# Causal attention and two MLPs on one core: a new order inside each pair of heads, and small [128 x 3..7] operations moved from VectorE to GpSimd

## The chip, the cores and the metric

The kernel runs on one core of one Trainium2 chip. The metric is the device time of one execution in microseconds (us). "Faster" or "slower" below is against the kernel before on the same chip.

## The reference

```python
scores = scale * np.matmul(q, k.transpose(0, 1, 3, 2))      # 2 x 12 heads, 448 x 448, head size 64
scores = np.where(mask, -1000000000.0, scores)              # causal
scores = scores - np.max(scores, axis=-1, keepdims=True)
attn = np.exp(scores)
attn = attn / (np.sum(attn, axis=-1, keepdims=True) + 1e-09)
attn_out = np.matmul(attn, v)
x = attn_out.transpose(0, 2, 1, 3).reshape(896, 768)
h = np.maximum(x @ w_in, 0.0);  x = h * h @ w_out            # 768 -> 2048 -> 768
h = x @ w_in2;  out = (h - np.tanh(h)) @ w_out2              # 768 -> 2048 -> 768
```

## The kernel before

**Attention.** The 24 heads are worked in 12 pairs (`NPAIR`). A pair `n` puts its two heads on the two halves of the 128 partitions. The 448 queries are cut into seven blocks `c` = 0 to 6 of 64; by causality block `c` has 64(c+1) keys. A pair goes through these steps, each a helper function:

- `scores(n, t)`, TensorE, in two parts. For pairs from 1 on, part 0 holds blocks 6, 5, 0 and part 1 blocks 3, 2, 4, 1 (`STEPS`); each part fills two PSUM banks. A bfloat16 product with `maskb` adds the causal mask (L281).
- `maxes(n, t)`, VectorE: one `tensor_reduce` per block (L292, minus the row maximum, into the small tile `st`), then one multiplication of the three or four maxima by 0.125 (L294). ScalarE's exponential reads that as its bias.
- `exps(n, t, z)`, ScalarE: `prob = exp(0.125 s + bias)` and the row sums (L301).
- `recips(n)`, VectorE: 1e-9 is added to the seven sums (L305), then the reciprocals (L306). `norms(n, cs)`, VectorE: each block of `prob` times its reciprocals, in place (L313).
- `transposes(n, t)`, t = 0 to 3: four 128x128 transposes on TensorE into one of two PSUM banks `t` (L321), and a ScalarE copy into `pt` (L322). By `TBLK`, t = 0 reads blocks 0 to 3, t = 1 blocks 4, 5, 6 and then 2, t = 2 blocks 3 to 6, t = 3 blocks 4, 5, 6, 6.
- `pv(n, kcs)`, TensorE: products with V for key chunks 0 to 3 (L334). `xhi` on ScalarE and `xlo` on VectorE split the result into a rounded part and a rest (L347, L351).

**The order is written out by hand.** Every engine executes its own instructions in the order in which the helpers are called; waits between engines come from the data. The loop over `s` (L463 on) works on three pairs at once: scores of pair `s`, softmax of pair `p = s - 1`, transposes and products of pair `a = s - 2`. Then a tail without a loop finishes pairs 10 and 11 between the first groups of matrix products of the first MLP (`first(0, 0, m, 0)`).

**Weight preparation.** The float64 weights arrive as 64-bit words and are turned into two float32r parts by four VectorE operations on 128x768 (L113, L118, L123, L132 or L134) and two on ScalarE (L103, L125) per unit. `one()` issues the next of these VectorE operations if the budget of the pair (`SHARE_PAIR`, 800) is not used up; it is called twice a pair. `late()` issues the ScalarE operations that they leave behind.

**The MLPs** follow: groups of 128x128 by 128x448 matrix products in three passes (L364 to L366), with the weights prepared along the way.

Of the kernel before, what the change touches and what calls it, by code (L numbers as in the profile page):

```python
# [8 lines left out]
F32 = mybir.dt.float32  # L9
# [13 lines left out]
P = 128  # L23
# [5 lines left out]
NQ = S // D  # L29
# [33 lines left out]
def body(ctx: ExitStack, tc: tile.TileContext, qT, kT, vL, w1, w2, w3, w4, out):  # L63
    nc = tc.nc
    sb = ctx.enter_context(tc.tile_pool(name="sb", bufs=1))
    ps = ctx.enter_context(tc.tile_pool(name="ps", bufs=1, space=PSUM))
# [7 lines left out]
    def slot(i, shape, dt, name):  # L74
        return sb.tile(shape, dt, tag=f"slot{i}", name=name)
# [75 lines left out]
    def room():  # L151
        i = len(taken) - RING
        return i < 0 or taken[i] < freed[0]
# [10 lines left out]
    def late():  # L164
        while act_late:
            act_late.pop(0)()

    def one():

        if todo and budget[0] > 0 and (room() or not todo[0][3]):  # L170
            take()
            return True

    def take():
        f, cost, _, _ = todo.pop(0)
        f()
        budget[0] -= cost
# [19 lines left out]
    def load_qk(n):  # L197
        if n < NPAIR:
            b, hp = divmod(n, NP)
            qk[n] = (tmp(f"q{n}"), tmp(f"k{n}", "w"))  # L200
            nc.sync.dma_start(out=qk[n][0], in_=qT[b, hp])
            (nc.scalar if n == 0 else nc.sync).dma_start(out=qk[n][1], in_=kT[b, hp])

    def load_v(b):
        t = sb.tile([P, 3, DM], F32, tag=f"v{b}", name=f"v{b}")
        nc.sync.dma_start(out=t, in_=vL[b, : 3 * P].rearrange("(t p) d -> p t d", p=P))
        if b == 0:
            vs["end"] = slot(7, [D, B, DM], F32, "vend")
            nc.sync.dma_start(out=vs["end"], in_=vL[:, 3 * P :].rearrange("b p d -> p b d"))
        vs[b] = [t[:, 0], t[:, 1], t[:, 2], vs["end"][:, b]]  # L210
# [5 lines left out]
    def warm(count):  # L216
        o = ps.tile([P, 512], F32, tag="o", bufs=2, name="warm")[:, :S]
        for _ in range(count):
            nc.tensor.matmul(o, lhsT=ones[:, :P], rhs=ones, start=True, stop=True)  # L219
# [33 lines left out]
    sc = {}  # L253
    stat = {}
    pt = {}
    ob = {}

    def step(n, t):

        return STEPS[1 - t if n == 0 else t]  # L260

    def scores(n, t):
        q, k = qk[n]
        banks = []
        for z, cs in enumerate(step(n, t)):
            bank = ps.tile([P, 512], F32, tag="s", bufs=4, name=f"s{n}_{t}_{z}")
            banks.append(bank)
            for c in cs:
                sc[n, c] = bank[:, SOFF[c] : SOFF[c] + D * (c + 1)]
        for i in range(2):  # L270
            for z, cs in enumerate(step(n, t)):
                for c in cs[i : i + 1]:
                    for j in range(2):
                        r, e = slice(D * j, D * j + D), D * (j ^ z)
                        nc.tensor.matmul(sc[n, c][e : e + D], lhsT=q[r, D * c : D * c + D], rhs=k[r, : D * (c + 1)], start=(c == cs[0]), stop=False, skip_group_check=True)  # L275
        for z, cs in enumerate(step(n, t)):
            d = [SOFF[c] // D + c for c in cs]
            o = banks[z].rearrange("p (b k) -> p b k", k=D)[:, d[0] : d[-1] + 1 : max(d[-1] - d[0], 1)]
            for j in range(2):
                r, e = slice(D * j, D * j + D), D * (j ^ z)  # L280
                nc.tensor.matmul(o[e : e + D], lhsT=identb[r, r], rhs=maskb[r, : len(cs)], start=False, stop=True, skip_group_check=True)  # L281
        if t == 1:
            qk.pop(n)
            load_qk(n + 3)

    def maxes(n, t):
        if t == 0:
            stat[n] = sb.tile([P, 3, 8], F32, tag="stat", bufs=3, name=f"st{n}")
        st = stat[n]
        cs = [c for b in step(n, t) for c in b]  # L290
        for c in cs:
            nc.vector.tensor_reduce(out=st[:, 0, SI[c] : SI[c] + 1], in_=sc[n, c], axis=AX.X, op=ALU.max, negate=True)  # L292
        a, z = SI[cs[0]], SI[cs[-1]] + 1
        nc.vector.tensor_scalar_mul(out=st[:, 0, a:z], in0=st[:, 0, a:z], scalar1=0.125)  # L294

    def exps(n, t, z):
        st = stat[n]
        for c in step(n, t)[z]:
            w = D * (c + 1)
            i = SI[c]  # L300
            nc.scalar.activation(prob[n % 3][:, POFF[c] : POFF[c] + w], sc.pop((n, c)), AF.Exp, bias=st[:, 0, i : i + 1], scale=0.125, accum_out=st[:, 1, i : i + 1])  # L301

    def recips(n):
        st = stat[n]
        nc.vector.tensor_scalar_add(out=st[:, 1, :NQ], in0=st[:, 1, :NQ], scalar1=1e-9)  # L305
        nc.vector.reciprocal(out=st[:, 2, :NQ], in_=st[:, 1, :NQ])  # L306

    def norms(n, cs):
        st = stat[n]
        for c in cs:  # L310
            i = SI[c]
            p = prob[n % 3][:, POFF[c] : POFF[c] + D * (c + 1)]
            nc.vector.tensor_scalar_mul(out=p, in0=p, scalar1=st[:, 2, i : i + 1])  # L313

    def transposes(n, t):
        if t == 0:
            pt[n] = slot(3 + n % 2, [P, 16, P], F32, f"pt{n}")
        bank = ps.tile([P, 512], F32, tag="t", bufs=2, name=f"t{n}_{t}")
        for i, (kc, c) in enumerate(TBLK[4 * t : 4 * t + 4]):
            o = bank.rearrange("p (i j q) -> p i j q", j=2, q=D)[:, i, :: -1 if c in TURNED else 1]  # L320
            nc.tensor.transpose(o, prob[n % 3][:, POFF[c] + P * kc : POFF[c] + P * kc + P], ident)  # L321
        nc.scalar.copy(out=pt[n][:, 4 * t : 4 * t + 4], in_=bank.rearrange("p (i q) -> p i q", q=P))  # L322

    def pv(n, kcs):
        b, hp = divmod(n, NP)
        if 0 in kcs:
            ob[n] = ps.tile([P, 512], F32, tag="o", bufs=2, name=f"o{n}")
        o = ob[n]
        for kc in kcs:
            r = P if kc < 3 else D  # L330
            m = NQ - 2 * kc
            for j in range(2):
                h = 2 * hp + j
                nc.tensor.matmul(  # L334
                    o[D * j : D * j + D, P * kc : S],
                    lhsT=vs[b][kc][:r, D * h : D * h + D],
                    rhs=pt[n][:r, TBASE[kc] : TBASE[kc] + m, D * j : D * j + D],
                    start=(kc == 0),
                    stop=(kc == 3),
                    skip_group_check=True,  # L340
                )
        if 3 in kcs:
            pt.pop(n)

    def xhi(n):
        b, hp = divmod(n, NP)
        nc.scalar.copy(out=x[hp][:, 0, b], in_=ob[n][:, :S])  # L347

    def xlo(n):
        b, hp = divmod(n, NP)  # L350
        nc.vector.tensor_sub(out=x[hp][:, 1, b], in0=ob.pop(n)[:, :S], in1=x[hp][:, 0, b])  # L351
# [111 lines left out]
    for s in range(NPAIR):  # L463
        p, a = s - 1, s - 2
        sp, sa = p >= 0, a >= 0
        budget[0] = min(budget[0], 0) + (SHARE_PAIR if s > 1 else 0)
        if sa:
            transposes(a, 0)
        if sp:
            maxes(p, 1)  # L470
            exps(p, 1, 0)
        if sa:
            transposes(a, 1)
        if sp:
            exps(p, 1, 1)
        one()
        if a >= 1:
            xhi(a - 1)
        scores(s, 0)
        maxes(s, 0)  # L480
        if sp:
            recips(p)
            norms(p, (3, 2))
        if s == 2:
            warm(5)
        if a >= 1:
            xlo(a - 1)
        if sa:
            transposes(a, 2)
            transposes(a, 3)  # L490
        exps(s, 0, 0)
        exps(s, 0, 1)
        if sp:
            norms(p, (1, 0, 4, 5, 6))
        if sa:
            pv(a, (0, 1))
        late()
        scores(s, 1)
        one()
        if sa:  # L500
            pv(a, (2, 3))
        if s == 1:
            load_v(1)

    p, a = NPAIR - 1, NPAIR - 2
    budget[0] = min(budget[0], 0) + SHARE_LAST
    transposes(a, 0)
    maxes(p, 1)
    exps(p, 1, 0)
    transposes(a, 1)  # L510
    exps(p, 1, 1)
    one()
    xhi(a - 1)
    act = first(0, 0, 0, 0)
    recips(p)
    norms(p, (3, 2))
    xlo(a - 1)
    transposes(a, 2)
    transposes(a, 3)
    act()  # L520
    norms(p, (1, 0, 4, 5, 6))
    act = first(0, 0, 1, 0)
    pv(a, range(4))
    late()
# [5 lines left out]
    act = first(0, 0, 2, 0)  # L530
    for t in range(4):
        transposes(p, t)
    act()
    pv(p, range(4))
    late()
# [57 lines left out]
```

## Time and profile before

| | |
|---|---|
| time of the kernel before, median of 3 runs | 568.91 us (567.93 to 569.95) |
| time of the profiled execution | 567.94 us |
| its span, first to last instruction | 566.2 us |
| busy PE, DVE, ACT, POOL in the span | 553.8, 405.6, 336.8, 1.8 us |
| granted TensorE clock | 1.00 throughout |

The profile is of one execution. PE is TensorE, DVE VectorE, ACT ScalarE, POOL GpSimd. A row of a timeline gives start and duration in us, engine, line, operation, what it writes and reads, and how many equal instructions it merges ("x4"); in brackets the idle time of the engine before it and what ended it. The chain of waits follows the last instruction back to what released it, step by step. Instructions that follow each other on one engine overlap a little, so durations of single ones add up to more than the time they take together.

### The profile page before, as it was taken

To read this page: it belongs to the slowest core of one execution; us is meant where nothing else is said; L and a number is where in the kernel's file an instruction comes from. 1 tells how busy PE (TensorE), PEld (TensorE's weight loads), DVE (VectorE), ACT (ScalarE), POOL (GpSimd) and SP (SyncE) were. 2 spreads that over 40 slices of the span, in tenths; PEclk is the share of its full clock that TensorE was granted. 3 is DMA by queue.
4 is the path that set the end of the run, shared out by engine and by line. 5 is a ranking of instruction groups with operands and counts; after the bars stand their busy time and mean duration, and the time that the engine had idled before them with its cause. 6 is when DMAs were issued, how large, how long until landed. Compare 5 with 4: busy or idle time off the path is not lost.

```text
span 566.2 us, 8063 instructions
## 1 busy us (share of the span) xinstructions
PE 553.8 (98%) x3134; PEld 479.5 (85%) x3134; DVE 405.6 (72%) x727; ACT 336.8 (59%) x650; POOL 1.8 (0%) x11
## 2 busy tenths in 40 slices
PE   6899999999999999999999999999999999999997
PEld 3455558899999999999999999999999999999996
DVE  5889995588667527665648579998887499898511
ACT  4798896777654336666424258786565487864100
POOL 1000000000000000000000000000000000000000
PEclk9999999999999999999999999999999999999999
DMA  8732301245355514333133330110665311015211
GB/s 279 296 123 66 107 1 57 59 164 167 113 168 167 168 56 168 111 112 111 57 112 112 111 113 1 56 56 11 214 218 172 118 50 56 1 57 184 81 49 49
DMA packets 15525, 61.85 MB, mean 109 GB/s; under 512 B 1664, under 2 KB 6400, under 8 KB 15488
## 3 DMA queue, kind: packets, MB, share of 16 engines
q1 hardware_dynamic: 15200, 61.00, 32.5%
q8 instruction: 24, 0.39, 0.3%
q10 hardware_dynamic: 288, 0.34, 0.2%
q14 instruction: 13, 0.11, 0.1%
HBM read 58.59 MB, written 2.75 MB: 108 GB/s over the span
## 4 chain that ended last, share of the span: by engine, by line
PE 90%; ACT 8%; DVE 2%; issue 0%; DVEq 0%; ACTq 0%
PE o L364 14%; PE o L365 14%; PE h L364 14%; PE o L366 14%; PE h L366 14%; PE h L365 14%; ACT p L301 4%; ACT pt L322 3%; PE o L334 3%; PE s L275 2%; PE t L321 1%; DVE st L292 1%; PE warm L219 1%; ACT x L347 1%; DVE p L313 0%
## 5 line engine op out<-in xcount | busy, mean ns | idle before, releaser
L364 PE MATMUL o<-g,w 128*128 128x448 f32 x384 | 141.3, 368 | 0.0
L365 PE MATMUL o<-g,w 128*128 128x448 f32 x384 | 141.2, 368 | 0.0
L366 PE MATMUL o<-g,w 128*128 128x448 f32 x384 | 140.3, 365 | 0.0
L364 PEld LDWEIGHTS o<-g,w 128*128 128x128 f32 x384 | 71.9, 187 | 7.2
L366 PEld LDWEIGHTS o<-g,w 128*128 128x128 f32 x384 | 72.1, 188 | 6.9
L125 ACT CAST w<-raw 128x768 fp32r<-128x768 f32 x64 | 57.9, 904 | 33.3 <-DVE raw L123 33.2
L365 PEld LDWEIGHTS o<-g,w 128*128 128x128 f32 x384 | 72.1, 188 | 6.4
L103 ACT ACTIVATE raw<-raw 128x768 f32<-128x768 f32 x64 | 59.3, 926 | 23.9 <-DMA raw<-w 23.9
L364 PE MATMUL h<-y,w 128*128 128x448 f32 x192 | 70.5, 367 | 0.0
L364 PE MATMUL h<-x,w 128*128 128x448 f32 x192 | 70.4, 367 | 0.0
L366 PE MATMUL h<-x,w 128*128 128x448 f32 x192 | 70.0, 365 | 0.0
L366 PE MATMUL h<-y,w 128*128 128x448 f32 x192 | 69.7, 363 | 0.0
L365 PE MATMUL h<-x,w 128*128 128x448 f32 x192 | 69.5, 362 | 0.0
L365 PE MATMUL h<-y,w 128*128 128x448 f32 x192 | 69.3, 361 | 0.0
L123 DVE SCALAR_TENSOR_TENSOR raw<-raw 128x768 int32<-128x768 int32 x64 | 61.2, 956 | 1.3
L118 DVE SCALAR_TENSOR_TENSOR raw<-raw 128x768 int32<-128x768 int32 x64 | 61.0, 953 | 0.9 <-ACT raw L103 0.9
L134 DVE TENSOR_TENSOR w<-raw,w 128x768 fp32r<-128x768 f32 x32 | 30.6, 958 | 28.0 <-ACT w L125 27.9
L373 DVE TENSOR_TENSOR g<-r,g 128x448 fp32r<-128x448 f32 x32 | 20.0, 625 | 37.8 <-ACT g L370 37.8
L301 ACT ACTIVATE p<-s,st 128x256 f32<-128x256 f32 (+6 forms) x84 | 40.1, 511 | 8.1 <-DVE st L294 7.0
L132 DVE SCALAR_TENSOR_TENSOR w<-w,raw 128x768 fp32r<-128x768 f32 x32 | 30.7, 959 | 18.7 <-ACT w L125 18.5
L366 PEld LDWEIGHTS h<-y,w 128*128 128x128 f32 x192 | 35.9, 187 | 3.5
L366 PEld LDWEIGHTS h<-x,w 128*128 128x128 f32 x192 | 36.0, 187 | 3.0
(57 smaller groups left out, 742.7 us busy)
## 6 DMA issues: line engine op xcount, KB each, us to landing
raw<-w SPq DMA_DIRECT2D x64, 768.0 KB, 4.3
q<-qT SPq DMA_DIRECT2D x12, 224.0 KB, 4.6
k<-kT SPq DMA_DIRECT2D x11, 224.0 KB, 3.1
out<-part SPq DMA_DIRECT2D x11, 224.0 KB, 1.9
v<-vL SPq DMA_DIRECT2D x2, 1152.0 KB, 10.1
vend<-vL SPq DMA_DIRECT2D x1, 384.0 KB, 10.0
k<-kT ACTq DMA_DIRECT2D x1, 224.0 KB, 3.5
out<-part ACTq DMA_DIRECT2D x1, 112.0 KB, 1.7
```

The lines of the kernel that those rows point to most:

```text
L103: nc.scalar.activation(h, h, AF.Copy, scale=2.0**-112)
L118: nc.vector.scalar_tensor_tensor(out=lo, in0=hi, scalar=3, in1=lo, op0=ALU.logical_shift_left, op1=ALU.bitwise_or)
L123: nc.vector.scalar_tensor_tensor(out=lo, in0=hi, scalar=-0x80000000, in1=lo, op0=ALU.bitwise_and, op1=ALU.bitwise_or)
L125: act_late.append(lambda: nc.scalar.copy(out=st["w"][:, 0], in_=lo.bitcast(F32)))
L132: nc.vector.scalar_tensor_tensor(out=w[:, 1], in0=w[:, 0].bitcast(F32), scalar=-(1.0 - 2.0**-24), in1=f, op0=ALU.mult, op1=ALU.add)
L134: nc.vector.tensor_sub(out=w[:, 1], in0=f, in1=w[:, 0])
L301: nc.scalar.activation(prob[n % 3][:, POFF[c] : POFF[c] + w], sc.pop((n, c)), AF.Exp, bias=st[:, 0, i : i + 1], scale=0.125, accum_out=st[ ...
L322: nc.scalar.copy(out=pt[n][:, 4 * t : 4 * t + 4], in_=bank.rearrange("p (i q) -> p i q", q=P))
L364: nc.tensor.matmul(h, lhsT=hi, rhs=xh, start=(k == 0), stop=False)
L365: nc.tensor.matmul(h, lhsT=hi, rhs=xl, start=False, stop=False)
L366: nc.tensor.matmul(h, lhsT=lo, rhs=xh, start=False, stop=(k == kk - 1))
L373: nc.vector.tensor_sub(out=dst[1], in0=v, in1=dst[0])
```

## The change

Within a pair the calls are put in another order. All products with V of pair `a` come in one run behind both parts of the scores. `transposes` is split: `transposes` holds the TensorE part, `tcopy` the ScalarE copy, and the four exponentials of part 1 now stand ahead of the first two copies. The products of blocks 4, 5, 6 with their reciprocals (`norms(a, (4, 5, 6))`) move to the next turn of the loop, behind `maxes(p, 1)`; the other four stand together behind `recips(p)`. `late()` moves ahead of the exponentials of part 0. The multiplication of the maxima by 0.125 and the addition of 1e-9 to the sums go to GpSimd.

```diff
@@ maxes
-        nc.vector.tensor_scalar_mul(out=st[:, 0, a:z], in0=st[:, 0, a:z], scalar1=0.125)
+        nc.gpsimd.tensor_scalar_mul(out=st[:, 0, a:z], in0=st[:, 0, a:z], scalar1=0.125)
@@ recips
-        nc.vector.tensor_scalar_add(out=st[:, 1, :NQ], in0=st[:, 1, :NQ], scalar1=1e-9)
+        nc.gpsimd.tensor_scalar_add(out=st[:, 1, :NQ], in0=st[:, 1, :NQ], scalar1=1e-9)
@@ the loop over pairs
-        if sa:
-            transposes(a, 0)
         if sp:
             maxes(p, 1)
-            exps(p, 1, 0)
         if sa:
+            norms(a, (4, 5, 6))
+            transposes(a, 0)
             transposes(a, 1)
         if sp:
+            exps(p, 1, 0)
             exps(p, 1, 1)
+        if sa:
+            tcopy(a, 0)
+            tcopy(a, 1)
         one()
         if a >= 1:
             xhi(a - 1)
         scores(s, 0)
         maxes(s, 0)
+        if s == 2:
+            warm(5)
         if sp:
             recips(p)
-            norms(p, (3, 2))
-        if s == 2:
-            warm(5)
+        if sa:
+            transposes(a, 2)
+            tcopy(a, 2)
+            transposes(a, 3)
+            tcopy(a, 3)
+        if sp:
+            norms(p, (1, 0, 2, 3))
+        late()
+        exps(s, 0, 0)
+        exps(s, 0, 1)
         if a >= 1:
             xlo(a - 1)
+        one()
+        scores(s, 1)
         if sa:
-            transposes(a, 2)
-            transposes(a, 3)
-        exps(s, 0, 0)
-        exps(s, 0, 1)
-        if sp:
-            norms(p, (1, 0, 4, 5, 6))
-        if sa:
-            pv(a, (0, 1))
-        late()
-        scores(s, 1)
-        one()
-        if sa:
-            pv(a, (2, 3))
+            pv(a, range(4))
@@ the tail
+    maxes(p, 1)
+    norms(a, (4, 5, 6))
     transposes(a, 0)
-    maxes(p, 1)
+    transposes(a, 1)
     exps(p, 1, 0)
-    transposes(a, 1)
     exps(p, 1, 1)
+    tcopy(a, 0)
+    tcopy(a, 1)
     one()
     xhi(a - 1)
     act = first(0, 0, 0, 0)
     recips(p)
-    norms(p, (3, 2))
...
-    norms(p, (1, 0, 4, 5, 6))
+    norms(p, (1, 0, 2, 3, 4, 5, 6))
```

How the instructions stand now is shown at three places of the turn `s` = 8 of the loop, where `s8` are the scores of pair 8, `st8` and `st7` the small tiles of pairs 8 and 7, `p1` the probabilities of pair 7, `t6`, `pt6` and `o6` the transposes, their copy and the product of pair 6. Lines of the changed kernel are some higher: L292 is L293 there, L306 L307, L313 L314, L321 L320, L334 L338, L351 L355.

VectorE, from the sums of pair 7 to the reduces of part 1 of pair 8, before:

```order
L305 TENSOR_SCALAR st7_751<-st7_751 128x7
L306 RECIPROCAL st7_751<-st7_751 128x7
L313 TENSOR_SCALAR p1_127<-p1_127,st7_751 128x256
L313 TENSOR_SCALAR p1_127<-p1_127,st7_751 128x192
L351 TENSOR_TENSOR x5_72<-o5_781,x5_72 128x448
L313 TENSOR_SCALAR p1_127<-p1_127,st7_751 128x128
L313 TENSOR_SCALAR p1_127<-p1_127,st7_751 128x64
L313 TENSOR_SCALAR p1_127<-p1_127,st7_751 128x320
L313 TENSOR_SCALAR p1_127<-p1_127,st7_751 128x384
L313 TENSOR_SCALAR p1_127<-p1_127,st7_751 128x448
L292 TENSOR_REDUCE st8_845<-s8_1_0_880 128x1 x2
L292 TENSOR_REDUCE st8_845<-s8_1_1_881 128x1 x2
```

and now:

```order
L307 RECIPROCAL st7_751<-st7_751 128x7
L314 TENSOR_SCALAR p1_127<-p1_127,st7_751 128x128
L314 TENSOR_SCALAR p1_127<-p1_127,st7_751 128x64
L314 TENSOR_SCALAR p1_127<-p1_127,st7_751 128x192
L314 TENSOR_SCALAR p1_127<-p1_127,st7_751 128x256
L355 TENSOR_TENSOR x5_72<-o5_797,x5_72 128x448
L293 TENSOR_REDUCE st8_845<-s8_1_0_872 128x1 x2
L293 TENSOR_REDUCE st8_845<-s8_1_1_873 128x1 x2
L314 TENSOR_SCALAR p1_127<-p1_127,st7_751 128x320
L314 TENSOR_SCALAR p1_127<-p1_127,st7_751 128x384
L314 TENSOR_SCALAR p1_127<-p1_127,st7_751 128x448
L132 SCALAR_TENSOR_TENSOR w1_737<-w1_737,raw1_122 128x768
```

The three widest products stand behind the reduces of part 1 instead of ahead of them, and the addition (L305) is gone from this queue.

TensorE, from the last transposes of pair 6 to the first of pair 7 (left out are the mask products), before:

```order
L321 MATMUL t6_3_861<-ident_63,p0_126 128x128 x2
L334 MATMUL o6_875<-pt6_809,v1_235 64x448 x2
L334 MATMUL o6_875<-pt6_809,v1_235 64x320 x2
L275 MATMUL s8_1_0_880<-k8_613,q8_612 64x256 x2
L275 MATMUL s8_1_1_881<-k8_613,q8_612 64x320 x2
L275 MATMUL s8_1_0_880<-k8_613,q8_612 64x192 x2
L275 MATMUL s8_1_1_881<-k8_613,q8_612 64x128 x2
...
L334 MATMUL o6_875<-pt6_809,v1_235 64x192 x2
L334 MATMUL o6_875<-pt6_809,vend_114 64x64 x2
L321 MATMUL t7_0_903<-ident_63,p1_127 128x2x64 x2
```

and now:

```order
L320 MATMUL t6_3_858<-ident_63,p0_126 128x128 x2
L276 MATMUL s8_1_0_872<-k8_605,q8_604 64x256 x2
L276 MATMUL s8_1_1_873<-k8_605,q8_604 64x320 x2
L276 MATMUL s8_1_0_872<-k8_605,q8_604 64x192 x2
L276 MATMUL s8_1_1_873<-k8_605,q8_604 64x128 x2
...
L338 MATMUL o6_890<-pt6_828,v1_232 64x448 x2
L338 MATMUL o6_890<-pt6_828,v1_232 64x320 x2
L338 MATMUL o6_890<-pt6_828,v1_232 64x192 x2
L338 MATMUL o6_890<-pt6_828,vend_114 64x64 x2
L320 MATMUL t7_0_907<-ident_63,p1_127 128x2x64 x2
```

The first half of the products with V has moved behind part 1 of the scores.

GpSimd had nothing in the loop; its queue now, in the same turn (the first row is the part 0 of pair 8, the next the sums of pair 7):

```order
L295 TENSOR_SCALAR st8_845<-st8_845 128x3
L306 TENSOR_SCALAR st7_751<-st7_751 128x7
L295 TENSOR_SCALAR st8_845<-st8_845 128x4
L295 TENSOR_SCALAR st9_940<-st9_940 128x3
L306 TENSOR_SCALAR st8_845<-st8_845 128x7
```

The addition to the sums of pair 7 (L306) stands behind the multiplication of the part-0 maxima of pair 8 (L295).

## Rows read from the trace of the kernel before

**Rows 1.** Busy time by stretch: start:end, length, then PE, PEld, DVE, ACT, POOL.

```profile
28.35:83.91 55.56, 52.91 (x548) 30.17 (x544) 50.77 (x162) 49.32 (x159) 0.00 (x0) 1.00 0.24 76
107.70:566.20 458.50, 455.10 (x2232) 418.27 (x2231) 321.56 (x464) 254.67 (x402) 0.00 (x0) 1.00 0.32 106
```

**Rows 2.** Chain that ended last, in order of time: start us, us, what.

```profile
64.43 0.59 ACT pt L322
65.02 0.87 ACT p L301 x4
...
68.19 0.76 PE o L334 x4
...
71.34 0.59 ACT pt L322
...
93.68 2.03 PE o L334 x16
```

**Rows 3.** Timeline of VectorE over one pair.

```profile
61.82 1.43 DVE L313 TENSOR_SCALAR p<-p,st 128x128 f32<-128x128 f32 x5
63.17 1.27 DVE L292 TENSOR_REDUCE st<-s 128x1 f32<-128x256 f32 x4
64.47 0.17 DVE L294 TENSOR_SCALAR st<-st 128x4 f32<-128x4 f32 x1
64.55 0.95 DVE L132 SCALAR_TENSOR_TENSOR w<-w,raw 128x768 fp32r<-128x768 f32 x1
65.80 1.22 DVE L292 TENSOR_REDUCE st<-s 128x1 f32<-128x448 f32 x3 [0.30 <-PE s L281]
67.06 0.17 DVE L294 TENSOR_SCALAR st<-st 128x3 f32<-128x3 f32 x1
67.27 0.17 DVE L305 TENSOR_SCALAR st<-st 128x7 f32<-128x7 f32 x1
67.47 0.20 DVE L306 RECIPROCAL st<-st 128x7 f32<-128x7 f32 x1
67.70 0.58 DVE L313 TENSOR_SCALAR p<-p,st 128x256 f32<-128x256 f32 x2
68.20 0.61 DVE L351 TENSOR_TENSOR x<-o,x 128x448 fp32r<-128x448 f32 x1
```

**Rows 4.** Timeline of TensorE in the same pair: transposes, then part 0 of the scores.

```profile
63.68 1.09 PE L321 MATMUL t<-ident,p 128*128 128x128 f32 x8
64.70 0.99 PE L275 MATMUL s<-k,q 64*64 64x448 f32 x12
```

**Rows 5.** Groups by form, VectorE, 28.35 to 83.91: xcount | busy us, mean ns | idle.

```profile
L313 DVE TENSOR_SCALAR p<-p,st 128x448 f32<-128x448 f32 x9 | 4.0, 446 | 0.0
...
L313 DVE TENSOR_SCALAR p<-p,st 128x128 f32<-128x128 f32 x8 | 2.2, 276 | 0.0
L313 DVE TENSOR_SCALAR p<-p,st 128x64 f32<-128x64 f32 x8 | 2.0, 248 | 0.0
```

**Rows 6.** Groups by form, GpSimd, whole span (same columns).

```profile
L229 POOL TENSOR_SCALAR_AFFINE_SELECT maskb<-maskb 64x64 bf16<-64x64 bf16 x4 | 0.9, 237 | 0.1
...
L586 POOL MEMSET const-float32-1.0<- 128x1 f32 x1 | 0.1, 99 | 0.0
```

**Rows 7.** Timeline of the first pair: a small VectorE operation and the exponential behind it.

```profile
6.91 0.17 DVE L294 TENSOR_SCALAR st<-st 128x4 f32<-128x4 f32 x1
...
7.17 0.47 ACT L301 ACTIVATE p<-s,st 128x256 f32<-128x256 f32 x1 [4.50 <-DVE st L294]
```

**Rows 8.** Timeline: part-1 reduces of pairs 3 and 11; the first MLP's first product.

```profile
28.35 1.28 DVE L292 TENSOR_REDUCE st<-s 128x1 f32<-128x256 f32 x4
...
83.91 1.28 DVE L292 TENSOR_REDUCE st<-s 128x1 f32<-128x256 f32 x4
...
85.27 0.45 PE L364 MATMUL h<-x,w 128*128 128x448 f32 x1
```

More of the change, by code (lines that the diff above doesn't have):

```diff
@@ L255, in body @@
     pt = {}
+    tb = {}
     ob = {}
@@ L315, in transposes @@
     def transposes(n, t):
-        if t == 0:
-            pt[n] = slot(3 + n % 2, [P, 16, P], F32, f"pt{n}")
-        bank = ps.tile([P, 512], F32, tag="t", bufs=2, name=f"t{n}_{t}")
+        bank = tb[n, t] = ps.tile([P, 512], F32, tag="t", bufs=2, name=f"t{n}_{t}")
         for i, (kc, c) in enumerate(TBLK[4 * t : 4 * t + 4]):
@@ L321, in transposes, with tcopy @@
             nc.tensor.transpose(o, prob[n % 3][:, POFF[c] + P * kc : POFF[c] + P * kc + P], ident)
+    def tcopy(n, t):
+        if t == 0:
+            pt[n] = slot(3 + n % 2, [P, 16, P], F32, f"pt{n}")
+        bank = tb.pop((n, t))
         nc.scalar.copy(out=pt[n][:, 4 * t : 4 * t + 4], in_=bank.rearrange("p (i q) -> p i q", q=P))
@@ L515, in body @@
     recips(p)
-    norms(p, (3, 2))
     xlo(a - 1)
     transposes(a, 2)
+    tcopy(a, 2)
     transposes(a, 3)
+    tcopy(a, 3)
     act()
-    norms(p, (1, 0, 4, 5, 6))
+    norms(p, (1, 0, 2, 3, 4, 5, 6))
     act = first(0, 0, 1, 0)
@@ L532, in body @@
         transposes(p, t)
+        tcopy(p, t)
     act()
```

## The prediction

> **What bounds the kernel now.** I first read the busy time by stretch. From 107.7 us on TensorE is busy 455.10 of 458.50 us [rows 1]; the change touches nothing there, so that part only shifts. What can change is the attention, above all its regular part: from the part-1 reduces of pair 3 to those of pair 11 [rows 8] lie eight turns in 55.56 us, 6.95 us each, in which no engine is full (PE 52.9, DVE 50.8, ACT 49.3 us) [rows 1]. A loop of waits sets the pace. The chain in order of time shows which: it repeats every 6.91 us (64.43 to 71.34), and runs from the copy of a transpose through exponentials and copies on ScalarE into the products with V, through the scores, and back to the transposes [rows 2]. Last I read VectorE's timeline over one such pair: it has work nearly all the time, and waits 0.30 us for the scores [rows 3]. So the old loop passes through ScalarE and TensorE; VectorE has little slack.
>
> **What the change cuts.** In that chain the products with V stand between the copies and part 1 of the scores [rows 2]. Now they stand behind it, so the old loop is open: part 1 of the scores no longer waits for the last copies. If nothing else closed, the pace would fall to what the fullest engine needs: PE 52.9 / 8 = 6.6 us.
>
> **What it closes instead.** VectorE's new queue makes a longer loop. I walk it once from the first part-1 reduce, each step with its row:
>
> 1. Four reduces: 1.27 us to the end of the last; the next instruction overlaps some 0.05: 1.22 [rows 3].
> 2. Products of blocks 4, 5, 6, now right behind. Five products take 1.43 us from the first start [rows 3]; the two small ones among them last 276 and 248 ns [rows 5] and overlap what follows by 0.08 (61.82 + 1.43 = 63.25 against 63.17), so they hold the queue for 0.20 and 0.17. That leaves 1.06 to the end of the widest.
> 3. The second group of transposes reads blocks 4, 5, 6 and then 2, and part 0 of the scores stands behind it on TensorE. Its third transpose waits for the widest product. Two transposes are left: eight take 1.02 to the start of the scores [rows 4], so 0.26; with one hop of 0.09 between engines (6.91 + 0.17 = 7.08, next start 7.17 [rows 7]): 0.35.
> 4. Scores, from their start to the first part-0 reduce: 64.70 [rows 4] to 65.80 [rows 3], 1.10. The weight operation of `one()` (0.95) [rows 3] lies beside steps 3 and 4 (1.45) and costs nothing; were they shorter, it would cost what sticks out.
> 5. Three reduces: 1.22 [rows 3].
> 6. The reciprocals now wait for GpSimd. Its queue holds the multiplication of these maxima, then the addition to the sums. The sums are ready long before, but the addition is queued behind a multiplication that waits for step 5. So VectorE stands still for two GpSimd operations and two hops: 2d + 0.18.
> 7. Reciprocal to first product 0.23 [rows 3]; four products 0.87 (0.50 for two [rows 3], 0.20 and 0.17 as above); the rest `xlo`, 0.61 less the overlap, 0.53 [rows 3]. Then the next part-1 reduces start.
>
> The sum is 1.22 + 1.06 + 0.35 + 1.10 + 1.22 + 0.18 + 0.23 + 0.87 + 0.53 = 6.76, and 2d. **GpSimd's d is not in the trace.** Its bounds: a memset of one column, which reads nothing, 0.099 us, and an affine select of 64 columns, which reads, computes and writes as this does, 0.237 us [rows 6]. For 3 to 7 columns I take 0.20, nearer to the operation of the same kind. A turn is then 7.16 us against 6.95: +0.21, eight times: **+1.7 us** (0.0 at 0.10, +2.3 at 0.24; GpSimd may also take longer than either).
>
> What left VectorE is small: three operations of 0.17 us a pair hold it, with their waits, for 0.08 + 0.21 + 0.20 [rows 3]. Step 6 gives back more than that.
>
> **The way into the tail.** From the part-1 reduces of pair 11 to the first MLP product took 1.36 us (83.91 to 85.27) [rows 8]. Now steps 1 to 3 stand there, 1.22 + 1.06 + 0.35 = 2.63, since that product is queued behind the same transposes. TensorE needs it too: all sixteen products with V (2.03) [rows 2] and eight transposes (1.02) are left when the scores end. That is **+1.3 us**, once. Behind it TensorE is full in both kernels.
>
> **The way in.** Pairs 0 to 2 win up to half the products with V, 1.0 us, as part 1 of the scores comes ahead of them; and lose GpSimd's time in exponentials that nothing covers, and 0.95 in turn 2, where `one()` gives a second weight operation, which now stands in the loop. I take 0, between -0.8 and +0.7.
>
> **What costs nothing.** The copies moved behind the exponentials: from the part-1 reduces, multiplication 0.09 + 0.20 + 0.09, four exponentials in two rows of 0.87 and two copies of 0.59 [rows 2], the last four transposes and the scores come to about 1.2 + 0.4 + 1.7 + 1.1 + 0.6 + 1.1 = 6.1, one microsecond inside 7.16. ScalarE's `late()` ahead of the part-0 exponentials uses that too (49.3 / 8 = 6.2 us of work a pair). The loads of q and k are issued with part 1 of the scores, three pairs ahead, as before; no queue of the DMAs is passed. The product's PSUM bank has been free for a turn when it is needed.
>
> **Sum:** 1.7 + 1.3 + 0 = +3.0 us. The profiled execution took 567.94 us, so it would be 570.9; it was 1 us faster than the median of 568.91, so as a median 572.0 (+0.5%).
>
> **A port that two engines share.** The products with reciprocals take (446 - 248) / 384 = 0.52 ns a column [rows 5], while the subtraction `xlo`, also float32, takes 0.61 us for 448 [rows 3], over twice as much a column: products run at a doubled rate. The part-1 multiplication on GpSimd now starts just as three of them start. The Trainium skill, "SBUF — State Buffer", section "SBUF: two separate sides", has it that GpSimd and a VectorE operation in a mode with two ports, or with two SBUF inputs, lock a shared pair of ports for a whole instruction, and the other is blocked. No run here shows it. By that rule, with the lock free at the end of the first product, the multiplication waits some 0.4 us, inside the one of slack, and the sum stays; held from one instruction to the next it is the second rival.
>
> **Rivals.**
>
> - *GpSimd is quick and the way in wins* (no change). With d = 0.10 a turn takes 6.96: 0.1 for eight, + 1.3 - 0.8 = +0.6, 569.5. For it speaks the short memset; against it that no operation that reads is that short [rows 6]. Chance 0.15.
> - *GpSimd is kept out while VectorE runs one SBUF operation after the other* (slower by more). The part-1 multiplication waits until the three products and the weight operation are through: 1.22 + 1.06 + 0.87 = 3.15, instead of 1.3, after the first reduce. The path of the copies, 6.1, becomes 7.9 or 8.0: +1.0 a turn, 8 in all, + 1.3 = +9.3, 578.2. It decides from a delay of one microsecond on; if only the products hold it (1.0), the sum stands. For it: the instructions overlap, so there is no gap between them [rows 3]. Against it: two turns in eight have a shorter weight operation. Chance 0.17.
> - *The reciprocals don't wait, or hardly* (faster): GpSimd works on its two small operations at once and hops in 0.03, so that step 6 costs 0.1 in all and the transposes overlap the products. A turn takes 6.65, PE's own 6.6 being the floor: -0.3 x 8 = -2.4, + 1.3 - 0.8 = -1.9, 567.0. It decides where step 6 is below some 0.15. For it: the memsets' rows are close together; against it: the queue's order, which puts two operations in a row there. Chance 0.11.
>
> The forecast itself, with d from 0.15 to 0.35, has 0.57.
>
> **How the numbers follow.** The likeliest is 572.0; its own range is 570.5 to 575. A measurement of this kernel can tell about 0.3%, 1.7 us, from no change. The range is to hold 0.8: it leaves out the fast rival and the upper half of the blocked one, so 569.0 to 578.5. Slower by over 0.3%: the forecast (0.57), the blocked rival (0.17), less 0.02 for a small d: 0.72. Within: 0.15 + 0.02 = 0.17. Faster: 0.11.
>
> **What would show it.** VectorE idle ahead of the reciprocal in each turn, released by GpSimd's addition, about 0.5 us; idle ahead of the part-0 reduces of some 0.5 us, released by the scores; part-1 reduces waiting for nothing; the turn near 7.16 us; GpSimd's two lines near 0.2 us. It is wrong if the reciprocal never waits, if the turn falls under 6.9, or if the exponentials of part 1 start more than two microseconds after their reduces end.

## The result, and the profile after

The changed kernel takes 574.49 us (median of 4 runs, 573.36 to 575.47) against 568.77 for the kernel before (4 runs, 567.93 to 569.95): 1.0102 times as long, 95% interval 1.0084 to 1.012. It is slower, as forecast, and inside the range; but it lost 5.7 us where 3.0 were forecast. Of its four executions only the profiled one had a mean granted clock of 1.0; the other three had 0.994 to 0.997 and took 0.7 to 2.1 us more (the last section returns to this).

The profiled execution took 573.36 us with a span of 571.6, against 567.94 and 566.2: +5.42 in time. First the two ends of the regular part, by VectorE's and TensorE's timelines of the changed kernel: the first reduces of pair 0, the part-1 reduces of pairs 3 and 11, and the first MLP product.

```profile
6.13 2.44 DVE L293 TENSOR_REDUCE st<-s 128x1 f32<-128x256 f32 x7 [2.44 <-PE s L282]
...
29.15 1.27 DVE L293 TENSOR_REDUCE st<-s 128x1 f32<-128x256 f32 x4
...
88.16 1.27 DVE L293 TENSOR_REDUCE st<-s 128x1 f32<-128x256 f32 x4
...
90.66 0.45 PE L368 MATMUL h<-x,w 128*128 128x448 f32 x1
```

The eight turns take 59.01 us, 7.38 each, where they took 55.56, 6.95 each [rows 8]: **+3.45**. Pair 3 begins 0.80 us later (29.15 against 28.35). From pair 11 to the first MLP product lie 2.50 us instead of 1.36: **+1.14**. Together 5.39, all of the longer time but 0.03; from there on the two kernels run alike.

Busy time by stretch (columns as in [rows 1]) says that the loss is waiting and not work:

```profile
29.15:88.16 59.01, 53.42 (x544) 31.77 (x542) 46.75 (x138) 49.25 (x159) 8.43 (x24) 1.00 0.22 70
```

TensorE and ScalarE were busy for nearly as long as in [rows 1] (TensorE 0.5 us longer), VectorE 4.0 us less, in 3.45 us more.

One turn, walked as the prediction walked it. VectorE's timeline:

```profile
58.66 1.27 DVE L293 TENSOR_REDUCE st<-s 128x1 f32<-128x256 f32 x4
59.85 1.07 DVE L314 TENSOR_SCALAR p<-p,st 128x320 f32<-128x320 f32 x3
60.83 0.56 DVE L113 TENSOR_SCALAR raw<-raw 128x768 int32<-128x768 int32 x1
62.44 1.22 DVE L293 TENSOR_REDUCE st<-s 128x1 f32<-128x448 f32 x3 [1.05 <-PE s L282]
64.40 0.20 DVE L307 RECIPROCAL st<-st 128x7 f32<-128x7 f32 x1 [0.74 <-POOL st L306]
64.64 0.94 DVE L314 TENSOR_SCALAR p<-p,st 128x128 f32<-128x128 f32 x4
65.50 0.62 DVE L355 TENSOR_TENSOR x<-o,x 128x448 fp32r<-128x448 f32 x1
```

and TensorE's, second transposes and part 0 of the scores:

```profile
59.69 1.72 PE L320 MATMUL t<-ident,p 128*128 128x128 f32 x8
61.34 0.99 PE L276 MATMUL s<-k,q 64*64 64x448 f32 x12
```

The next part-1 reduces start at 66.03, so this turn has 7.37 us. In [rows 3] VectorE had two small operations and a reciprocal between the part-0 reduces and the products. Now it stands still there for 0.74 us, in every turn. The waits over the eight turns show this, and that VectorE's part-0 reduces wait for the scores and TensorE's transposes for VectorE's products (who waited for whom: us in total, times, longest; PEld is TensorE's weight load):

```profile
DVE st L293 <- PE s L282: 6.0, 8, 1.1
DVE st L307 <- POOL st L306: 5.9, 8, 0.7
PEld t L320 <- DVE p L314: 1.8, 8, 0.2
```

The chain in order of time shows what fills the 0.74 us (start, us, what):

```profile
62.46 1.21 DVE st L293 x3
63.67 0.02 issue
63.69 0.02 POOLq L295
63.71 0.10 issue
63.81 0.23 POOL st L295
64.04 0.08 issue
64.12 0.26 POOL st L306
64.38 0.02 issue
64.40 0.21 DVE st L307
```

The sums of the previous pair were ready long before; what VectorE waits for is GpSimd's queue, where their addition (L306) stands behind the multiplication of the maxima (L295) that have just been reduced. GpSimd by form (xcount | busy us, mean ns | idle):

```profile
L295 POOL TENSOR_SCALAR st<-st 128x4 f32<-128x4 f32 x12 | 6.3, 527 | 38.4 <-DVE st L293 38.4
L306 POOL TENSOR_SCALAR st<-st 128x7 f32<-128x7 f32 x12 | 3.0, 247 | 2.8 <-ACT p L302 1.9
L295 POOL TENSOR_SCALAR st<-st 128x3 f32<-128x3 f32 x12 | 2.8, 229 | 36.5 <-DVE st L293 36.5
```

Four columns take more than twice as long as three or seven. In pair 0, before any product, the 128x4 took 0.24 us; in ten of the other eleven 0.58. The timelines of GpSimd and ScalarE in the turn above:

```profile
60.01 0.58 POOL L295 TENSOR_SCALAR st<-st 128x4 f32<-128x4 f32 x1 [3.02 <-DVE st L293]
...
60.62 0.47 ACT L302 ACTIVATE p<-s,st 128x256 f32<-128x256 f32 x1 [0.87 <-POOL st L295]
```

It starts inside the first of VectorE's three widest products and ends at 60.59, right behind the second (60.55). The exponential that waits for it starts 0.03 later, so the long duration is no error of the record.

### The profile page after: what moved, and what is told of

It is laid out like the page before. It is cut to its first block, busy times and chain, and to the rows that moved or that the text cites. A ratio compares the mean times of both kernels' runs of the same rounds, so it can differ in the third digit from the quotient of the medians.

```text
span 571.6 us, 8095 instructions
## 1 busy us (share of the span) xinstructions
PE 556.5 (97%) x3134; PEld 482.4 (84%) x3134; DVE 399.7 (70%) x691; ACT 337.3 (59%) x650; POOL 13.8 (2%) x47
## 4 chain that ended last, share of the span: by engine, by line
PE 90%; DVE 5%; ACT 3%; POOL 1%; issue 1%; DVEq 0%; ACTq 0%; POOLq 0%
PE o L368 14%; PE o L369 14%; PE h L368 14%; PE o L370 14%; PE h L370 14%; PE h L369 13%; PE t L320 3%; DVE st L293 3%; PE o L338 2%; PE s L276 2%; ACT p L302 1%; DVE p L314 1%; ACT pt L326 1%; PE warm L219 1%; POOL st L295 1%
## 5 line engine op out<-in xcount | busy, mean ns | idle before, releaser
L320 PE MATMUL t<-ident,p 128*128 128x128 f32 x192 | 33.0, 290 | 9.2 <-ACT pt L326 5.3
```

## The experiments

The kernel before took 568.28 us beside e1 to e4, 568.63 beside e5 to e8 and 568.61 beside e9 and e10; ratios are against these. A turn is, as above, an eighth of the way from the part-1 reduces of pair 3 to those of pair 11. Diffs are against the changed kernel.

### Which of the two moved operations costs, and what the order costs alone

e1 puts the addition back on VectorE, e2 the multiplication, e3 both.

```diff
@@ e1, e3
-        nc.gpsimd.tensor_scalar_add(out=st[:, 1, :NQ], in0=st[:, 1, :NQ], scalar1=1e-9)
+        nc.vector.tensor_scalar_add(out=st[:, 1, :NQ], in0=st[:, 1, :NQ], scalar1=1e-9)
@@ e2, e3
-        nc.gpsimd.tensor_scalar_mul(out=st[:, 0, a:z], in0=st[:, 0, a:z], scalar1=0.125)
+        nc.vector.tensor_scalar_mul(out=st[:, 0, a:z], in0=st[:, 0, a:z], scalar1=0.125)
```

> The addition of 1e-9 goes back to VectorE, the multiplication stays on GpSimd. Queue theory (the reciprocals wait behind two GpSimd operations in a row, 0.74 us a turn in the changed kernel's trace): the wait goes, an addition of 0.20 comes, so a turn falls from 7.38 to 7.38 - 0.74 + 0.20 = 6.84 us and the time by 8 x 0.54 = 4.3 to about 570.2 us. Rival 1, the blocked multiplication of part 1 (0.58 instead of 0.23 us) and the exponentials behind it set the turn: the turn stays at 7.38 and the time at 574.5. Rival 2, the order alone is slow: the turn stays above 7.2 and the time above 573.

> The multiplication goes back to VectorE, the addition stays on GpSimd, where nothing stands ahead of it any more. Queue theory: no wait of the reciprocals; the two multiplications hold VectorE for 0.08 and 0.21 us a turn as in the kernel before: 7.38 - 0.74 + 0.29 = 6.93 us, time lower by 8 x 0.45 = 3.6, about 570.9 us. Rival 1 (exponentials behind a blocked GpSimd): also lower, the exponentials of part 1 start some 0.9 us earlier; e1 tells the two apart. Rival 2 (the order alone): above 573 us.

> The new order alone, nothing on GpSimd. Queue theory with the loop through VectorE as worked out: 7.38 - 0.74 + 0.29 + 0.20 = 7.13 us a turn, time lower than the changed kernel's by 8 x 0.25 = 2.0, about 572.5 us, so the order alone is some 0.2 us a turn slower than the kernel before. Rival 3 (all of the loss is GpSimd's): the turn is at or under 6.95 us and the time at or under 570.7 (the way into and out of the loop cost 1.9 us in the changed kernel).

Measured: e1 569.47 us (1.0019, 1.0010 to 1.0029), turn 6.81; e2 570.09 (1.0037, 1.0023 to 1.0050), turn 6.93; e3 573.05 (1.0087, 1.0072 to 1.0102), turn 7.14. VectorE's timeline of e1 at the reciprocals:

```profile
60.80 1.22 DVE L293 TENSOR_REDUCE st<-s 128x1 f32<-128x448 f32 x3 [1.12 <-PE s L282]
61.94 0.16 DVE L306 TENSOR_SCALAR st<-st 128x7 f32<-128x7 f32 x1
62.13 0.20 DVE L307 RECIPROCAL st<-st 128x7 f32<-128x7 f32 x1
62.37 0.94 DVE L314 TENSOR_SCALAR p<-p,st 128x128 f32<-128x128 f32 x4
```

The wait is gone, and with it 0.57 us of the turn: from the start of the reduces to the reciprocal it takes 1.33 us by way of VectorE's own addition, and took 1.96 by way of GpSimd. The three turns are within 0.03 us of those expected; the times of e1 and e2 lie 0.7 and 0.8 us below the expected ones, that of e3 0.6 above. e3 shows that the new order itself is 0.19 us a turn slower than the old one, and that moving both operations adds 0.24 to that. Against e3 each operation moved alone is a gain: 0.33 us a turn for the multiplications (e1) and 0.21 for the addition (e2), about what they hold VectorE in the loop (0.29 and 0.20). It is both together, in this order of the queue, that cost.

### Both on GpSimd, the addition ahead (e4)

```diff
-    def recips(n):
+    def sums(n):
         st = stat[n]
         nc.gpsimd.tensor_scalar_add(out=st[:, 1, :NQ], in0=st[:, 1, :NQ], scalar1=1e-9)
+
+    def recips(n):
+        st = stat[n]
         nc.vector.reciprocal(out=st[:, 2, :NQ], in_=st[:, 1, :NQ])
@@ the loop
         scores(s, 0)
+        if sp:
+            sums(p)
         maxes(s, 0)
@@ the tail
     act = first(0, 0, 0, 0)
+    sums(p)
     recips(p)
```

> Both stay on GpSimd, but the addition to the sums of pair p is queued ahead of the multiplication of the part-0 maxima of pair s; nothing else moves. Queue theory: the sums are ready 0.9 us before those maxima, so the wait of 0.74 us goes entirely: 7.38 - 0.74 = 6.64 us, or what then sets the turn: the path over the blocked multiplication, exponentials, copies, transposes and scores takes 65.24 - 58.66 = 6.6 us in the changed kernel's trace. So 6.65 to 6.85 us, time lower by 4.2 to 5.8: 568.7 to 570.3 us. Rival 1 (the blocked multiplication decides) and rival 2 (the order): 7.2 us a turn or more, 573 us or more.

Measured: 567.12 us (0.9979, 0.9969 to 0.9988), turn 6.68. The turn is as expected, the time 1.6 us below the expected range; in the profiled execution pair 3 begins at 28.37, not at 29.15. Timelines of VectorE and GpSimd:

```profile
59.05 1.22 DVE L293 TENSOR_REDUCE st<-s 128x1 f32<-128x448 f32 x3 [1.05 <-PE s L282]
60.19 0.19 DVE L310 RECIPROCAL st<-st 128x7 f32<-128x7 f32 x1
```

```profile
59.15 0.25 POOL L306 TENSOR_SCALAR st<-st 128x7 f32<-128x7 f32 x1 [1.94 <-ACT p L302]
60.43 0.31 POOL L295 TENSOR_SCALAR st<-st 128x3 f32<-128x3 f32 x1 [1.03 <-DVE st L310]
```

The addition starts under the reduces, 1.04 us ahead of the reciprocal, which follows the last reduce at once. The operations and their engines are those of the changed kernel, with durations that differ by less than 0.1 us in these rows (0.31 against 0.23 for the multiplication); what was changed is a place in a queue, and it is worth 0.7 us a turn. Against e3 the two moves now gain 0.46, near the sum of their single gains (0.54). This settles the term of step 6.

### What VectorE's operations do to GpSimd's (e5, e6, e9)

e5 keeps both operations on GpSimd and takes the order of the kernel before. There the part-1 multiplication falls beside a weight operation instead of the products.

```diff
@@ the loop, as before; maxes and recips as changed
+            transposes(a, 0)
         if sp:
             maxes(p, 1)
+            exps(p, 1, 0)
...
-            norms(a, (4, 5, 6))
-            transposes(a, 0)
...
             recips(p)
+            norms(p, (3, 2))
```

> The order of the kernel before, with the multiplication and the addition on GpSimd. Queue theory: the addition again stands behind the multiplication of the part-0 maxima, so the reciprocals start 0.15 + 0.23 + 0.08 + 0.25 + 0.03 = 0.74 us after the reduces where they started 0.45 us after them (67.02 to 67.47): +0.3 us a turn, of which VectorE's slack of 0.30 us hides most; and the part-1 multiplication runs beside a weight operation instead of three products. If that blocks it to the end of the weight operation (0.55 or 0.95 us), the exponentials of part 1, which are on the old loop's chain, start 0.3 to 0.7 us later. So 7.2 to 7.6 us a turn, 571 to 574 us. Rival 3 (GpSimd alone is the loss of the change, whatever the order): 6.95 + 0.43 = 7.38, 572 to 574.5 as well; rival (GpSimd costs nothing in the old order, as VectorE has slack there): 6.95, 568.3 us.

Measured: 576.54 us (1.0141, 1.0116 to 1.0166), turn 7.49: the turn is as expected, the time above it. Pair 3 begins at 31.52 in the profiled execution, 3.2 us later than before, with the granted clock at 0.62 and 0.53 in the rows from 14 to 18 us, and at 0.53 and 0.61 in those from 28 to 32 (more on this at the end). One turn in the timelines of VectorE, GpSimd and ScalarE:

```profile
69.92 0.95 DVE L132 SCALAR_TENSOR_TENSOR w<-w,raw 128x768 fp32r<-128x768 f32 x1
...
70.08 0.89 POOL L294 TENSOR_SCALAR st<-st 128x4 f32<-128x4 f32 x1 [4.00 <-DVE st L292]
...
71.01 0.47 ACT L301 ACTIVATE p<-s,st 128x256 f32<-128x256 f32 x1 [0.55 <-POOL st L294]
```

The multiplication starts 0.16 us after a weight operation with two SBUF inputs, whose record ends at 70.87, and lasts 0.89, to 70.97. In eleven turns it took 0.87 to 0.89 beside such an operation and 0.47 to 0.50 beside the shift L113 (0.56 us), and in pair 0, beside neither, 0.24. This is what the Trainium skill, "SBUF — State Buffer", section "SBUF: two separate sides", says of the pair of ports that the two engines share: whoever starts first has it for the whole instruction, and operations with two SBUF inputs count as well as those in a two-port mode. The trace agrees, with one addition: next to VectorE instructions that follow each other without a gap, GpSimd did get in (0.30 or 0.58 us beside three products of 1.07), so it was never kept out for a whole run of them.

e6 puts all seven products behind the reciprocals in the new order, so that the part-1 multiplication meets a weight operation there too; e9 does the same with the multiplication on VectorE.

```diff
@@ e6, e9
         if sa:
-            norms(a, (4, 5, 6))
             transposes(a, 0)
...
-            norms(p, (1, 0, 2, 3))
+            norms(p, (1, 0, 2, 3, 4, 5, 6))
@@ e9
-        nc.gpsimd.tensor_scalar_mul(out=st[:, 0, a:z], in0=st[:, 0, a:z], scalar1=0.125)
+        nc.vector.tensor_scalar_mul(out=st[:, 0, a:z], in0=st[:, 0, a:z], scalar1=0.125)
```

> All seven products stand together behind the reciprocals, none behind the part-1 reduces; there VectorE now does the weight operation at once. A test of the shared port: the part-1 multiplication on GpSimd, 0.58 us beside three products at double rate, should take 0.23 us where VectorE reads PSUM or rests, and last until the weight operation ends where one is running: some 0.5 us beside the shift (L113, 0.55 us, one input), 0.9 us beside those with two inputs (0.95 us) if they block it as well, 0.23 if they do not. If GpSimd's operation took 0.58 us for another reason than what runs beside it (its four columns, say), it stays at 0.58 in every turn. The turn is not the point: 6.9 to 7.7 us.

> All seven products behind the reciprocals, as in the run before with that order (turn 8.33 us, one look 583.0), with one thing changed: the multiplication of the maxima is on VectorE again, and the addition stays on GpSimd. If that order lost its time because GpSimd's multiplication lasts up to 0.88 us beside the weight operation and so holds up the exponentials, the copies behind them and the products with V: VectorE's multiplication comes right behind the reduces, before the weight operation, and the turn falls by 0.6 us or more, to 7.0 to 7.7, 573 to 578 us. If the order alone lost it (seven products ahead of the part-1 reduces, with TensorE and ScalarE waiting for them), the turn stays above 8.0 and the time above 580 us.

Measured, one execution each: e6 583.01 us, turn 8.33; e9 568.66 us, turn 7.10. In e6 GpSimd's multiplication took 0.87 to 0.88 us beside the weight operations with two inputs and 0.47 to 0.48 beside the shift, as expected if the port is locked; four columns as the reason for 0.58 is refuted. But e6's turn missed its expectation by far. e9's turn is in its expected range, its time 4 us below it. ScalarE's waits in the eight turns, e6 (waited for: us in total, times, longest):

```profile
ACT p L302 <- POOL st L295: 16.2, 7, 3.6
```

and e9:

```profile
ACT p L302 <- DVE st L295: 6.4, 6, 1.5
```

With the multiplication on GpSimd this order is 1.2 us a turn slower (8.33 against 7.10), and ScalarE, with its exponentials and all copies queued behind it, waits 9.8 us longer in eight turns. That is not the price of the multiplication alone. The addition again stands behind a multiplication in e6, and the granted clock falls four times within its eight turns (busy time in rows of 2 us; the column ahead of the last two is the clock):

```profile
42.00:44.00 2.00, 1.38 (x12) 1.06 (x16) 1.40 (x7) 2.00 (x7) 0.45 (x2) 0.96 0.95 375
44.00:46.00 2.00, 2.00 (x22) 1.31 (x16) 1.76 (x6) 1.95 (x7) 0.00 (x0) 0.50 0.21 76
46.00:48.00 2.00, 2.00 (x12) 0.76 (x8) 1.64 (x4) 0.23 (x1) 0.87 (x1) 0.69 0.72 222
```

TensorE had stood still for 2.07 us before 42.62, waiting for a copy of ScalarE. Over the last seven of e6's turns the mean granted clock is 0.89 to 0.91, and they take 7.4 to 7.5 and 9.5 to 9.6 us by turns; e9's clock is 1.00 throughout. A tenth of those 58.5 us is some 6 us, an estimate of the most that the fallen clock can make of the 9.8. How the 1.2 us divide between multiplication, addition and clock these two runs do not tell. In e6's first turn, with the clock at 1.00, the difference is 0.70 (8.13 against 7.43). The order alone, with the addition on GpSimd (e9), costs 0.15 against before. In the changed kernel the multiplication is delayed by 0.35 us, and the path of the copies has room for that: the part-1 reduces wait for nothing.

### Past both kernels (e7, e8, e10)

In e4's turn VectorE still waits 1.05 us for the scores, which on TensorE stand behind transposes that wait for the widest product. e7 is e4 with part 0 of the scores ahead of those; e8 has that order, with the multiplication on VectorE and the addition alone on GpSimd.

```diff
@@ e7, e8
             transposes(a, 0)
+        scores(s, 0)
+        if sa:
             transposes(a, 1)
...
-        scores(s, 0)
```

> e4 (addition queued first), and on TensorE part 0 of the scores stands ahead of the second group of transposes, so that it no longer waits for the three widest products. Loop theory: steps 2 and 3 leave VectorE's loop (its wait for the scores, 1.05 us beside a shift, goes); what is left is TensorE's own work, 52.9 / 8 = 6.6 us a turn, and the path over the part-1 multiplication: 6.55 to 6.7 against 6.68 in e4. Time 565.5 to 567.2 us. If the products' place was not on any loop after e4: as e4, 567.1.

> As e7, but with the multiplication on VectorE and only the addition on GpSimd, where nothing is ahead of it. No GpSimd operation is left between maxima and exponentials, so these start some 0.5 us earlier than in e4; VectorE pays 0.29 us a turn, of which it has 1 us to spare once it doesn't wait for the scores. Turn 6.5 to 6.7 us, time 565 to 567 us; if the port's 0.35 us was never on a path, as e7.

Measured: e7 565.11 us (0.9936, 0.9917 to 0.9955), e8 563.93 (0.9919, 0.9902 to 0.9936), turns 6.56 in both: the turns are as expected, the times a little below. e7's busy time in the eight turns:

```profile
26.49:79.00 52.51, 51.30 (x546) 31.61 (x548) 46.73 (x137) 49.71 (x158) 6.83 (x24) 1.00 0.25 80
```

TensorE is busy 51.30 of 52.51 us (51.00 of 52.51 in e8): it is the bound now, and on which engine the multiplication runs makes no difference to the turn. **These two beat both kernels**, e8 by 4.7 us against before and by some 10 against the changed one. Part 0 of the scores ahead of the transposes is worth 0.12 us a turn with both operations on GpSimd (e4 to e7) and 0.37 with the addition alone there (e2 to e8).

e10 is e8 with more dummy products on TensorE in the first turns.

```diff
@@ on top of e8
+        if s == 2:
+            warm(5)
         scores(s, 0)
...
-        if s == 2:
-            warm(5)
...
         scores(s, 1)
+        if s == 0:
+            warm(4)
```

> The fastest order so far (scores first, multiplication on VectorE, addition on GpSimd), with four more dummy products on TensorE behind the scores of pair 0, and the five of turn 2 moved ahead of its part-0 scores, where TensorE had stood still until the clock fell to 0.50 in several profiles. Theory: the clock stays at 1.00 through the first 24 us in every execution, no run lies near the 567.9 us of the one that fell, and the median is what the executions at 1.00 took, 563.8 to 564.6 us. Rival: the clock falls all the same, or the dummy products hold up the scores that stand behind them, by up to 1.1 us: 565 us or more, with executions that differ by 3 us.

Measured: 564.75 us (0.9931, 0.9910 to 0.9952), six executions between 563.77 and 565.67, with a mean granted clock of 0.999 or 1.0 in each. The clock stayed up, and no execution lies near 567.9; but the median is no better than e8's 563.93, and slightly above the range that the theory named. What the dummies save in some executions they seem to take in all; 0.8 us between two medians whose executions overlap doesn't settle more.

## Why the prediction was right, and where its sizes were off

**Sign and mechanism.** The loop it walked is the loop of the trace: VectorE waits for the scores ahead of the part-0 reduces, for GpSimd's addition ahead of the reciprocals, and not at all ahead of the part-1 reduces. By its steps, forecast and measured in the turn from 58.66: step 1 1.22 and 1.19; step 2 1.06 and 1.07; step 3 0.35 and 0.42; step 4 1.10 and 1.10; step 5 1.22 and 1.22; **step 6 0.58 and 0.74**; step 7 1.63 and 1.63. The sum was 7.16 and is 7.37.

**The step that was mis-sized** is step 6, "2d + 0.18" with d = 0.20. The two operations take 0.23 and 0.26 us, near the affine select that the prediction had as the upper of its bounds [rows 6] and passed over; and the hops are not two of 0.09 [rows 7] but 0.14 from VectorE to GpSimd, 0.08 between GpSimd's two operations and 0.02 back: 0.24 with d = 0.245. Step 3 adds 0.07, step 1 takes back 0.03. Since all this lies on the path eight times, the 0.21 us a turn that the walk lacks became 1.7 in all: most of the 2.4 us that the sum missed (5.4 in the profiled executions against 3.0). The rest is the way in, less 0.16 of the tail.

**The way into the tail**, forecast +1.3, came to +1.14, as the prediction had it: TensorE has its products with V and transposes left when the scores end, and stands still only within the eight transposes ahead of that product, which take 1.72 us (from 89.19) instead of 1.09.

**The way in**, forecast 0 within -0.8 and +0.7, was +0.80, just outside its bounds. The first reduces of pair 0 start 0.54 us later (6.13 against 5.59), but that is made up for by pair 1. The part-1 reduces of pairs 1 and 2 before:

```profile
13.70 1.28 DVE L292 TENSOR_REDUCE st<-s 128x1 f32<-128x256 f32 x4
...
21.68 1.28 DVE L292 TENSOR_REDUCE st<-s 128x1 f32<-128x256 f32 x4
```

and in the changed kernel:

```profile
13.69 1.28 DVE L293 TENSOR_REDUCE st<-s 128x1 f32<-128x256 f32 x4
...
21.77 1.28 DVE L293 TENSOR_REDUCE st<-s 128x1 f32<-128x256 f32 x4
```

Up to pair 2 the change costs 0.09 us, near the forecast 0. The other 0.71 come between pairs 2 and 3: that turn takes 7.38 us already (21.77 to 29.15), the pace of the eight behind it, and took 6.67 before (21.68 to 28.35), less than the eight there. In e4, with the addition queued ahead, the same turn takes 6.54 (21.83 to 28.37). So the new loop was walked nine times and not eight; the sum counted the ninth as way in, at no cost.

**The rivals.** A quick GpSimd (d = 0.10) is refuted by its rows. That the reciprocals hardly wait is refuted as well, though it comes true with the addition in another place: e4's turn of 6.68 and its 567.12 us are near the 6.65 and 567.0 that this rival named. A GpSimd kept out over a run of VectorE operations was not seen; the lock is held by the instruction. In another order a loss of more than the size that it named appears, in e6, where the multiplication meets a weight operation of 0.95 us; how much of that loss is the multiplication's is open, as said above.

**"What costs nothing."** That the copies' path had room to spare held: the multiplication delayed by 0.35 us (the prediction's estimate by the port was 0.4) and 49.25 us of ScalarE's work fitted in. How much room was left was not measured. The sign that GpSimd's lines would be near 0.2 us failed for this one operation alone.

## What to carry to other kernels

An operation moved to an idle engine takes a place in that engine's queue: before moving two, read in the order of instructions what stands ahead of each, for an operation whose input is ready early must not stand behind one whose input comes late. A small operation on GpSimd cost its duration (0.23 to 0.25 us here), two hops (0.16 together), and up to 0.65 us more where it met a VectorE instruction. Whether that pays depends on the path: in the changed kernel's order, where VectorE's queue is the loop, moving the multiplications alone gained 0.33 us a turn (e1 against e3); with the scores first it made no difference (e7, e8); and where the multiplication met the weight operations, with all exponentials behind it, it went with a loss (e6 against e9). An order that opens one loop closes another: walk the new one, from its first turn on, and put ahead in each queue what the next engine waits for.

## What the runs showed of the hardware that was not expected

**The granted clock fell in the first 24 us**, in some executions and not in others. In e3's profile (2 us per row; the column ahead of the last two is the clock):

```profile
6.00:8.00 2.00, 0.20 (x12) 0.04 (x4) 1.97 (x7) 0.94 (x5) 0.00 (x0) 1.00 0.90 335
...
12.00:14.00 2.00, 0.73 (x4) 0.45 (x4) 1.97 (x10) 1.07 (x6) 0.00 (x0) 0.96 1.05 352
14.00:16.00 2.00, 1.48 (x6) 0.78 (x9) 1.05 (x4) 1.83 (x9) 0.00 (x0) 0.50 1.04 421
16.00:18.00 2.00, 2.00 (x17) 1.04 (x18) 0.33 (x1) 0.95 (x2) 0.00 (x0) 0.50 0.99 409
```

TensorE had been busy for 0.20 us between 6 and 8 and 0.73 between 12 and 14, and then ran at the lower level, 1.2 GHz, until past 20 us. The profiles of before and of the changed kernel show 1.00 throughout, though before too was busy for only 0.32 and 1.02 us in those rows; e8's profiled execution fell in the same way and took 567.87 us, its four others, at a mean of 1.00, 563.77 to 564.62. So such a fall goes with up to some 4 us here, more than two thirds of what the whole change lost. The profiles of e1 to e5 show a fall too, ahead of their eight turns, and few executions of those runs had a mean clock of 1.0: one of ten of e1, two of ten of e4, none of e2, e3 and e5; of the kernel before, beside e1 to e4, all twenty had 0.999 or 1.0. So a part of these runs' times is this and not the steady turn. Executions with a mean of 1.0 took 573.36 us with the change, 567.97 in e1, 566.32 and 566.40 in e4. In e5 and e6 the clock fell later as well, after TensorE had waited within the turns (in e5 it was busy for 0.71 us from 24 to 26, and the clock was 0.53 from 28 to 30). e10's rows show TensorE busy for 2.00 us from 6 to 8 and 1.30 from 12 to 14, and the clock at 1.00. That the dummies kept it there is not shown: four of e8's five executions had no fall without them, and the changed kernel's profile shows 1.00 with TensorE busy for only 0.73 us from 12 to 14 and 0.82 from 14 to 16.

**The lock between VectorE and GpSimd was one-sided here**: the three products took 1.07 us with GpSimd's multiplication beside them as in e2 without it, so that it was GpSimd that waited. In these cases VectorE had started first; no row shown here has the other order.
